# Attention: two chunks' tails transposed into one bank, a fourth p tile, merged tail evictions, another table of turns

## The chip, the cores and the metric

One core of one Trainium2 chip. The metric is the device time of one launch in microseconds (us). Three runs of the kernel before gave 1039.3 to 1040.34 us, median 1039.94 us.

## The reference, cut to what matters

Four batches of eight heads, 576 positions, head size 64, all float32; then two dense blocks.

```python
def _attn_ref(q, k, v, tau):
    scores = q @ k.T / sqrt(64)                       # per head, 576 x 576
    thresh = max(scores, -1) - tau
    scores = where(scores >= thresh, scores, -1e9)
    attn = exp(scores - max(scores, -1))
    attn = attn / (sum(attn, -1) + 1e-9)
    return attn @ v
x = attention output as (4 * 576, 512)
h = x @ w_in;  g = max(h, 0) + alpha * min(h, 0);  x = g @ w_out      # d_ff 2048
x = (((x @ w1) * (x @ w2)) @ w3) @ w_out2                              # d_ff 1024
```

The weights of the dense blocks come as float64 and are turned into float32 on the chip by integer operations.

## The kernel before, in words

The kernel has two stages, each written out by a planner in Python as one fixed list of instructions per engine. The first, attention, ends near 306 us; the dense stage fills the rest. The change touches the first, and of the second only where two weight tiles lie.

Attention goes over 16 pairs of heads (P). The 576 queries of a pair are cut into chunks of 128: chunks 0 to 3 for each of the two heads (units 0 to 7, chunk c of head h is unit 2c+h), and the last 64 queries of both heads together as unit 8. A step has a letter and a number:

- a, b, c, d: load of q or k, split into two fp32r parts on GpSimd (POOL), transposition on TensorE (PE; cq, ck, and ctails for the last 64 positions of both), eviction on ScalarE (ACT; dq, dk, dtails; prep_ev, lines 304 to 331). dswap makes the second form of q by two DMAs.
- Q: four matmuls of scores (eight for unit 8) into one of three two-bank PSUM tiles "s", which cq and ck use too. R: row maximum on VectorE (DVE). H: threshold. E: exp on ACT. M: mask and multiply on DVE into a p tile, of which there are NPB = 3; M frees the s tile.
- G (POOL) and I (DVE): the reciprocal of the sum. C: scaling of p on POOL, in place.
- T: transposition of p on PE, with the PSUM tag "ptp" (two banks) that ctails and V use too. Chunk c has three groups: g = 0 and 1, four blocks of 128 columns for either head, and g = 2, the one block that holds the last 64 columns of both heads. Txg is named after the chunk's second unit: T10, T11, T12 for chunk 0, T30.. for chunk 1, T50.. for 2, T70.. for 3, T80 and T82 for unit 8. X: its eviction on ACT (trans_ev, lines 493 to 509).
- V0, V1: 20 matmul calls of p against v for chunks 0 and 1, then for chunks 2, 3 and the last 64. Y: eviction into xT.
- w0 to w8: conversion of 14 tiles of w_in in the shade of attention: w0 load (512 KB on the SP queue, one buffer), w1 on ACT, w2 to w5 on DVE, w6 on POOL, w7 on ACT, w8 on POOL.

Each step has a number in the table AT (line 578); its turn is that number plus PER times the pair. turn_order (lines 87 to 118) takes, of the steps whose inputs are already in the list, the one of the lowest turn; a step that takes a tile waits in it until the tile's former holder is freed. Every engine runs its part of this list in order, and so does the SP queue with its DMAs.

SBUF: xT and the 16 tiles "wa" lie on the left, the attention pool on the right. That pool is closed after attention, and the dense stage's buffers ("raw" among them) take its place.

Of the kernel before, what the change touches and what calls it, by code (L numbers as in the profile page):

```python
# [120 lines left out]
def kernel(  # L121
# [99 lines left out]
    with tc.manual_schedule():  # L221
# [26 lines left out]
        for i in range(2):  # L248
# [83 lines left out]

# [1205 lines left out]
```

## Time and profile before

| | |
|---|---|
| median of three runs | 1039.94 us |
| the profiled execution | 1039.72 us |
| its span, first to last instruction | 1037.9 us |
| PE, DVE, ACT, POOL busy | 1014.1, 751.6, 580.6, 340.1 us |
| mean granted clock of TensorE | 0.998 |

The page gives busy time over the whole span, which hides that two stages are added up; the views by window below show the attention stage alone. A PE record holds the time until the matmul's modelled end, so that records of PE overlap; on DVE and ACT the records of neighbours overlap too, and what one more instruction costs is the distance of two starts.

### The profile page before, as it was taken

Reading aid. Unit: us, or ns where it says so; the run is one execution under the profiler, and the core shown is the slowest. Engines: PE = TensorE matmul, PEld = TensorE weight load, DVE = VectorE, ACT = ScalarE, POOL = GpSimd, SP = SyncE. Lnnn points to the kernel's source line nnn. Section 1 sums busy time; section 2 is a strip of 40 time slices with the busy share of each in tenths; the row PEclk is TensorE's granted clock in tenths of the full one; section 3 lists DMA queues with packets and bytes.
Section 4 is the critical chain, followed back from the end, with each engine's and each line's share of the span. In section 5 each row is a group of like instructions: output and inputs, shape, how many; then the busy total and the mean of one; then the engine's idle time right before and its main releaser. Section 6 shows DMA issues by size and latency. Waiting matters only on the chain.

```text
span 1037.9 us, 16931 instructions
## 1 busy us (share of the span) xinstructions
PE 1014.1 (98%) x5870; PEld 867.0 (84%) x5870; DVE 751.6 (72%) x1556; ACT 580.6 (56%) x1119; POOL 340.1 (33%) x469
## 2 busy tenths in 40 slices
PE   8999999999989999999999999999999999999997
PEld 6778777777858889988888888888899999999997
DVE  7999999999858787667656565638475587577554
ACT  5998989999865665544443344324143363345331
POOL 4888888888733232222211211103200000000000
PEclk9999999999999999999999999999999999999999
DMA  5353443435113333434524233512242233224201
GB/s 128 90 141 100 131 112 117 125 89 153 39 41 104 112 110 114 141 117 156 176 80 142 104 136 106 172 41 72 92 139 75 81 108 122 71 72 148 91 11 61
DMA packets 71445, 109.50 MB, mean 106 GB/s; under 512 B 14912, under 2 KB 43584, under 8 KB 71360
## 3 DMA queue, kind: packets, MB, share of 16 engines
q1 hardware_dynamic: 68992, 108.16, 33.3%
q8 instruction: 46, 0.75, 0.3%
q10 hardware_dynamic: 2368, 0.27, 0.2%
q14 instruction: 39, 0.32, 0.1%
HBM read 80.22 MB, written 18.35 MB: 95 GB/s over the span
## 4 chain that ended last, share of the span: by engine, by line
PE 87%; POOL 5%; issue 2%; DVE 2%; ACT 2%; DMA 1%; SPq 0%; POOLq 0%; ACTq 0%; DVEq 0%
PE h L985 25%; PE acc L985 24%; PE h L1341 17%; PE pv_ps L518 8%; PE pt_ps L491 5%; PE s_ps L402 5%; POOL p L474 3%; PE tr L291 2%; POOL ks L181 1%; POOL qs L181 1%; PE zero L352 1%; PE h L858 1%; DMA raw<-in_moe_w_dram 0%; POOL praw L474 0%; ACT qT L311 0%
## 5 line engine op out<-in xcount | busy, mean ns | idle before, releaser
L985 PE MATMUL h<-x,wa 128*128 128x512 f32 (+1 forms) x960 | 212.4, 371 | 1.1 <-ACT x L183 1.1
L985 PE MATMUL acc<-gs,wu 128*128 128x512 f32 (+1 forms) x960 | 209.8, 368 | 0.4 <-DVE wu L829 0.4
L985 PEld LDWEIGHTS h<-x,wa 128*128 128x128 f32 x960 | 167.3, 189 | 32.6 <-ACT x L183 3.0
L985 PEld LDWEIGHTS acc<-gs,wu 128*128 128x128 f32 x960 | 168.1, 189 | 31.0 <-DVE wu L829 0.8
L1341 PE MATMUL h<-T,sw 128*128 128x384 f32 x1008 | 190.6, 336 | 0.0
L1341 PEld LDWEIGHTS h<-T,sw 128*128 128x128 f32 x1008 | 178.4, 188 | 8.3
L218 POOL TENSOR_TENSOR m<-m,raw 128x512 int32<-128x512 int32 x58 | 81.6, 1408 | 281.5 <-DVE m L213 213.9
L1405 DVE TENSOR_TENSOR ct<-h,ct 128x384 f32<-128x384 f32 x120 | 66.8, 557 | 91.6 <-PE h L1341 91.5
L426 DVE TENSOR_REDUCE sm<-s_ps 128x1 f32<-128x576 f32 x144 | 105.6, 751 | 13.2 <-PE s_ps L402 13.1
L437 ACT ACTIVATE e<-s_ps,sm 128x576 f32<-128x576 f32 x144 | 106.0, 764 | 7.4 <-DVE sm L426 4.7
L474 POOL TENSOR_SCALAR p<-p,sm 128x576 f32<-128x576 f32 x128 | 96.7, 762 | 26.8 <-DVE sm L467 17.7
L451 DVE SCALAR_TENSOR_TENSOR p<-s_ps,sm,e 128x576 f32<-128x576 f32 x128 | 102.6, 811 | 0.8 <-ACT e L437 0.8
L183 ACT CAST gs<-g 128x512 fp32r<-128x512 f32 (+1 forms) x80 | 46.2, 577 | 94.2 <-PE acc L985 77.5
L491 PE MATMUL pt_ps<-ident,p 128*128 128x128 f32 x576 | 87.3, 280 | 11.3 <-ACT pt L505 8.7
L188 DVE TENSOR_TENSOR gs<-g,gs 128x512 fp32r<-128x512 f32 (+1 forms) x80 | 60.0, 750 | 47.0 <-ACT gs L183 46.4
L1056 ACT ACTIVATE g<-h,sign_sb 128x512 f32<-128x512 f32 (+1 forms) x80 | 51.3, 642 | 69.5 <-PE h L985 62.2
L1061 DVE SCALAR_TENSOR_TENSOR g<-h,salpha_sb,g 128x512 f32<-128x512 f32 (+1 forms) x80 | 55.6, 694 | 47.3 <-ACT g L1056 47.2
L491 PEld LDWEIGHTS pt_ps<-ident,p 128*128 128x128 f32 x576 | 66.0, 142 | 26.5 <-POOL praw L474 10.5
L518 PE MATMUL pv_ps<-pt,vraw 128*64 128x256 f32 (+1 forms) x640 | 84.7, 411 | 0.3 <-ACT xT L531 0.2
L183 ACT CAST sw<-w 128x512 fp32r<-128x512 f32 (+1 forms) x96 | 54.0, 569 | 55.4 <-PE h L1341 53.6
L505 ACT COPY pt<-pt_ps 128x512 f32<-128x512 f32 x128 | 74.5, 596 | 15.6 <-PE pt_ps L491 14.6
L985 PE MATMUL acc<-wp,x 128*128 128x512 f32 x288 | 81.9, 394 | 0.0
(121 smaller groups left out, 1521.3 us busy)
## 6 DMA issues: line engine op xcount, KB each, us to landing
raw<-in_moe_w_dram SPq DMA_DIRECT2D x32, 512.0 KB, 3.7
raw<-in_moe_w_out_dram SPq DMA_DIRECT2D x24, 512.0 KB, 3.5
w<-w SPq DMA_DIRECT2D x48, 256.0 KB, 2.6
qU<-qT SPq DMA_DIRECT2D x30, 320.0 KB, 4.0
w<-w SPq DMA_DIRECT2D x24, 384.0 KB, 2.9
wraw<-in_moe_w_in_dram SPq DMA_DIRECT2D x14, 512.0 KB, 3.8
w<-m SPq DMA_DIRECT2D x24, 256.0 KB, 2.1
z<-w SPq DMA_DIRECT2D x24, 256.0 KB, 2.7
```

The costliest lines, as they stand in the source:

```text
L183: eng.copy(out=dst, in_=src)
L218: nc.gpsimd.tensor_tensor(out=mc[0], in0=mc[0], in1=mc[1], op=ALU.add)
L426: nc.vector.tensor_reduce(out=sm_of(u, 0), in_=st[u], axis=AX.XY, op=ALU.max, negate=True)
L437: nc.scalar.activation(out=es[u].rearrange("p (j s) -> p j s", j=2), in_=st[u], func=AF.Exp, bias=sm_of(u, 0))
L451: nc.vector.scalar_tensor_tensor(out=p_at(u).rearrange("p (j s) -> p j s", j=2), in0=st.pop(u), scalar=sm_of(u, 1), in1=es.pop(u).rearrang ...
L474: nc.gpsimd.tensor_scalar(out=out, in0=in_, scalar1=sm_of(u, 3), scalar2=1.0, op0=ALU.mult, op1=ALU.mult)
L491: nc.tensor.transpose(t[:, i, :], p[:, at + i * 128 : at + (i + 1) * 128], ident)
L505: nc.scalar.copy(out=pt[:, g, 0:4, to], in_=ps)
L518: nc.tensor.matmul(out=o[64 * hh : 64 * hh + 64, 0:n], lhsT=vr[:, hh, i, :], rhs=pt[:, 0 if i == 4 and not half else hh, i, :], start=(i = ...
L985: nc.tensor.matmul(out=out, lhsT=l, rhs=r, start=first and i == 0, stop=last and i == n - 1)
L1341: nc.tensor.matmul(out=bank_()[:, 0:HT], lhsT=w()[:, ap_, kc * 128 : kc * 128 + 128], rhs=x()[:, bp, kc * HT : kc * HT + HT], start=first ...
L1405: lambda e: ENG[e].tensor_tensor(out=dst(), in0=x(), in1=y(), op=how),
```

## The change

Five edits, and a sixth that follows from the second:

1. The blocks g = 2 of chunks 0 and 1 (and of 2 and 3) are transposed in one step into one bank, and evicted by one copy (128x256, or 128x512 with the doubling) where there were two. T12, X12, T52, X52 are gone; T32 waits for the scaling of chunks 0 and 1, T72 for that of 2 and 3.
2. NPB is 4.
3. dtails: one copy for q (128x128) and one scaled copy for k (128x256), where there were two each.
4. w2 of the 14 tiles goes from DVE to ACT.
5. AT has other numbers.
6. "wa" has 14 tiles; the two last w_in tiles of the dense stage lie in a pool "w_b" opened after attention at the place of the two dropped.

```diff
-    w_a = wa_ctx.enter_context(tc.tile_pool(name="w_a", bufs=16, reuse_waits="tile"))
+    w_a = wa_ctx.enter_context(tc.tile_pool(name="w_a", bufs=14, reuse_waits="tile"))
...
-        NPB = 3
+        NPB = 4
...
-                for h in range(2):
-                    nc.scalar.copy(
-                        out=d["qT"][:, h, SM + ST * h : SM + ST * h + ST],
-                        in_=ps[:, 0, ST * h : ST * h + ST].bitcast(F32),
-                    )
-                for at in (0, S):
-                    nc.scalar.activation(
-                        out=d["kT"][:, :, at : at + ST],
...
+                nc.scalar.copy(out=tails(d["qT"])[:, SM // ST :: SM // ST + 3, :], in_=by_head(ps[:, 0, :]))
+                nc.scalar.activation(
+                    out=d["kT"].rearrange("p h (b s) -> p h b s", s=ST)[:, :, :: S // ST, :],
+                    in_=by_head(ps[:, 1, :]).unsqueeze(2).to_broadcast([128, 2, 2, ST]),
+                    func=AF.Copy,
+                    scale=kscale,
+                )
...
+            if g == 2:
+                for i, c_ in enumerate((c,) if c == 4 else (c - 1, c)):
+                    nc.tensor.transpose(t[:, i, :], p_of[P, c_][:, SM : SM + 128], ident)
+                return
...
-            elif half == 0:
-                nc.scalar.copy(out=pt[:, 0, 4, to], in_=ps[:, 0])
             else:
-                nc.scalar.copy(out=pt[:, :, 4, to], in_=ps[:, 0].unsqueeze(1).to_broadcast([128, 2, 128]))
+                two = ps[:, 0:2].rearrange("p i s -> p (i s)")
+                if half == 0:
+                    nc.scalar.copy(out=pt[:, 0, 4, 0:256], in_=two)
+                else:
+                    nc.scalar.copy(out=pt[:, :, 4, 0:256], in_=two.unsqueeze(1).to_broadcast([128, 2, 256]))
...
-                    "V",
+                    "V" if i else "A",
                     lambda e, f=f, i=i: high_w_in(e, f, i),
...
+        w_b = wa_ctx.enter_context(tc.tile_pool(name="w_b", bufs=2, reuse_waits="tile"))
```

The two tables are too long to print. What they come to, by the rule of turn_order, is this order per frame (one pair's worth of steps in the steady part; b is the pair before a, n the one after, z the one before b; in the new table PER is unchanged and 14 frames carry w steps, two pairs later than before):

```
before  PE    V1z T10b Q6b T11b Q7b T50b T12b Q0a T52b T51b Q8a T80b T82b Q4a T32b T30b Q1a T31b T70b Q5a T71b V0b cq_n T72b ctails_n Q2a Q3a ck_n
after   PE    V1z Q7b T50b T51b Q0a T11b T31b Q8a T32b T30b Q1a T80b T82b Q4a T72b T70b Q5a V0b ctails_n cq_n ck_n T71b Q2a Q3a T10a Q6a
after   DVE   R7b H6 M6 R0a H0 H7 M7b R8a I7b M0a w5 H8 M8a R1 H1 R4 H4 R5 M1 M4 I1 H5 M5 I8 R2 R3 H3 I5 R6 H2 M2 M3 w3 w4 I3
after   ACT   Y1z X50b X51b E7b X11b X31b E0a X32b X30b E8a X80b X82b X72b X70b w7 E1 E4 E5 Y0b dtails_n dq_n dk_n X71b E2 X10a E3 w2 w1 E6a
after   POOL  C8b G7b C7b C6b w6 bk_n (4) G8a G1a C0a C1a G5a w8 bq (4, the pair after n) C4a C5a G3a C3a C2a
after   SP    aq, w0, dswap_n, v_n, ak (the pair after n)
```

## Rows read from the trace of the kernel before

**Rows 1.** Busy time of each engine in one frame (--windows; columns in the first line)

```profile
core 0: us, PE busy (x) PEld busy (x) DVE busy (x) ACT busy (x) POOL busy (x), PEclk, DMA share, GB/s
136.00:154.00 18.00, 17.29 (x141) 14.08 (x140) 17.03 (x46) 16.33 (x36) 15.54 (x26) 1.00 0.42 117
```

**Rows 2.** Chain that ended last, in one frame: start us, us, what

```profile
138.94 0.54 PE s_ps L402 x4
139.48 0.87 PE pt_ps L491 x8
...
141.32 2.31 PE pv_ps L518 x20
143.63 0.81 PE tr L291 x8
...
145.83 0.65 PE tr L291 x8
```

**Rows 3.** Chain that ended last: first V0, V0 of pair 14, last V1

```profile
33.40 2.31 PE pv_ps L518 x20
...
284.60 2.31 PE pv_ps L518 x20
...
303.64 2.94 PE pv_ps L518 x20
```

**Rows 4.** Timeline, DVE in one frame: start us, us, engine line op

```profile
145.33 1.42 DVE L426 TENSOR_REDUCE sm<-s_ps 128x1 f32<-128x576 f32 x2 [0.71 <-PE s_ps L402]
...
147.23 0.51 DVE L207 TENSOR_SCALAR m<-m 128x512 f32<-128x512 f32 x1
...
148.52 0.32 DVE L429 TENSOR_SCALAR sm<-sm,ctau 128x1 f32<-128x1 f32 x2
...
149.57 0.69 DVE L213 SCALAR_TENSOR_TENSOR m<-wraw,m 128x512 int32<-128x512 int32 x1
...
152.60 0.82 DVE L451 SCALAR_TENSOR_TENSOR p<-s_ps,sm,e 128x576 f32<-128x576 f32 x1
...
153.34 0.21 DVE L429 TENSOR_SCALAR sm<-sm,ctau 128x1 f32<-128x1 f32 x1
...
153.47 0.75 DVE L426 TENSOR_REDUCE sm<-s_ps 128x1 f32<-128x576 f32 x1
```

**Rows 5.** Groups by line, 0 to 345 us: count, busy us, mean ns, idle before

```profile
L313 ACT ACTIVATE kT<-tr,kscale 128x1024 fp32r<-128x1024 f32 x16 | 18.6, 1159 | 0.7 <-PE tr L291 0.7
...
L311 ACT CAST qT<-tr 128x1024 fp32r<-128x1024 f32 x16 | 16.3, 1016 | 9.9 <-PE tr L291 9.9
...
L509 ACT COPY pt<-pt_ps 128x256 f32<-128x256 f32 x32 | 12.4, 387 | 0.0
...
L507 ACT COPY pt<-pt_ps 128x128 f32<-128x128 f32 x32 | 8.9, 279 | 0.4 <-PE pt_ps L491 0.4
...
L204 DVE TENSOR_SCALAR m<-wraw 128x512 int32<-128x512 int32 x14 | 7.4, 529 | 0.4 <-DMA wraw<-in_moe_w_in_dram 0.4
...
L202 ACT ACTIVATE m<-raw 128x512 f32<-128x512 f32 x8 | 5.3, 661 | 0.0
```

**Rows 6.** Timeline, ACT and POOL instructions that follow without a gap

```profile
139.96 1.08 ACT L505 COPY pt<-pt_ps 128x512 f32<-128x512 f32 x2 [0.38 <-PE pt_ps L491]
...
140.92 2.02 ACT L437 ACTIVATE e<-s_ps,sm 128x576 f32<-128x576 f32 x3
...
142.31 1.55 POOL L188 TENSOR_TENSOR ks<-kraw,ks 128x256 fp32r<-128x256 f32 x2
...
153.79 1.47 POOL L474 TENSOR_SCALAR p<-p,sm 128x576 f32<-128x576 f32 x2
```

**Rows 7.** Timeline, start of the dense stage: the same DVE form beside POOL and alone

```profile
310.79 0.43 DVE L209 TENSOR_SCALAR m<-m 128x512 int32<-128x512 int32 x1
...
312.18 1.30 POOL L218 TENSOR_TENSOR m<-m,raw 128x512 int32<-128x512 int32 x1 [14.02 <-DVE m L213]
312.31 1.45 DVE L209 TENSOR_SCALAR m<-m 128x512 int32<-128x512 int32 x1
```

**Rows 8.** DMA issues on the page: KB each, median us to landing

```profile
wraw<-in_moe_w_in_dram SPq DMA_DIRECT2D x14, 512.0 KB, 3.8
```

More of the change, by code (lines that the diff above doesn't have):

```diff
@@ L487, in trans @@
             t = pt_ps[P, c, g] = ps_a.tile([128, 4, 128], F32, tag="ptp", name="pt_ps", bufs=2)
+            if g == 2:
+                for i, c_ in enumerate((c,) if c == 4 else (c - 1, c)):
+                    nc.tensor.transpose(t[:, i, :], p_of[P, c_][:, SM : SM + 128], ident)
+                return
             p = p_of[P, c]
-            at = (0, S + ST, SM)[g]
-            for i in range(1 if g == 2 else 4):
+            at = (0, S + ST)[g]
+            for i in range(4):
                 nc.tensor.transpose(t[:, i, :], p[:, at + i * 128 : at + (i + 1) * 128], ident)
@@ new lines @@
+        AT = {'aq_0': 57.932, 'bq0hi_0': -5.26462375720813e+233, 'bq0lo_0': -5.26462375720813e+233, 'bq1hi_0': -5.264623757208129e+233, 'bq1lo_0': -5.264623757208129e+233, 'ak_0': 72.92, 'bk0hi_0': 0.526, 'bk0lo_0': -5.264623757208129e+233, 'bk1hi_0': 6.578, 'bk1lo_0': -1.7211269975488118e+233, 'cq_0': 21.681, 'dq_0': -3.479850037031599e+233, 'ctails_0': 113.869, 'dtails_0': -5.200977034580411e+233, 'ck_0': 124.257, 'dk_0': -5.200977034580411e+233, 'eq': 125.223, 'fq': -5.264623757208129e+233, 'etails': 130.148, 'ftails': 140.709, 'v': 131.775, 'Q0': -20.437, 'R0': 134.255, 'H0': -5.26462375720813e+233, 'E0': -5.200977034580411e+233, 'M0': 136.284, 'Q1': 130.138, 'R1': 138.618, 'H1': -5.264623757208129e+233, 'E1': -5.200977034580411e+233, 'M1': 140.689, 'G1': -1128612512929.835, 'I1': 141.951, 'C0': -1128612513286.866, 'C1': -1128612513124.268, 'T10': 145.941, 'X10': -8.744473794239729e+233, 'T11': 152.259, 'X11': -5.200977034580411e+233, 'Q2': 145.25, 'R2': -5.26462375720813e+233, 'H2': 149.291, 'E2': -5.200977034580411e+233, 'M2': -5.26462375720813e+233, 'Q3': 145.874, 'R3': 146.402, 'H3': 140.522, 'E3': -5.200977034580411e+233, 'M3': -1.7211269975488118e+233, 'G3': -1128612513645.092, 'I3': 151.42, 'C2': 154.089, 'C3': -1128612513643.817, 'T30': 130.66, 'X30': -5.200977034580411e+233, 'T31': 153.127, 'X31': -5.200977034580411e+233, 'T32': 126.195, 'X32': -5.200977034580411e+233, 'V0': 161.753, 'Y0': -5.200977034580411e+233, 'Q4': 130.67, 'R4': 138.658, 'H4': -5.264623757208129e+233, 'E4': -5.200977034580411e+233, 'M4': 141.226, 'Q5': 130.827, 'R5': 140.629, 'H5': 142.561, 'E5': -5.200977034580411e+233, 'M5': -6.985750754756941e+233, 'G5': -1128612512933.779, 'I5': 146.948, 'C4': -1128612513642.171, 'C5': -1128612513477.898, 'T50': 150.728, 'X50': -5.200977034580411e+233, 'T51': 130.128, 'X51': -5.200977034580411e+233, 'Q6': 148.891, 'R6': -5.264623757208129e+233, 'H6': 153.805, 'E6': -5.200977034580411e+233, 'M6': 5.684, 'Q7': 150.608, 'R7': 152.245, 'H7': 154.281, 'E7': -5.200977034580411e+233, 'M7': -5.264623757208129e+233, 'G7': 155.923, 'I7': -5.264623757208129e+233, 'C6': 156.493, 'C7': -1128612513645.102, 'T70': 127.236, 'X70': -5.200977034580411e+233, 'T71': 164.241, 'X71': -8.744473794239729e+233, 'T72': 126.185, 'X72': -5.200977034580411e+233, 'Q8': 123.723, 'R8': 134.922, 'H8': 138.246, 'E8': -5.200977034580411e+233, 'M8': -5.264623757208129e+233, 'G8': -1128612512580.549, 'I8': 143.079, 'C8': 155.831, 'T80': 114.406, 'X80': -3.479850037031599e+233, 'T82': 150.618, 'X82': -5.200977034580411e+233, 'V1': 168.997, 'Y1': -5.200977034580411e+233, 'aq': 87.91, 'bq0hi': -1128612512927.751, 'bq0lo': -1128612513123.155, 'bq1hi': -1128612512933.769, 'bq1lo': -1128612512739.518, 'ak': 117.955, 'bk0hi': -1128612514737.118, 'bk0lo': -1128612513308.768, 'bk1hi': -1128612513645.112, 'bk1lo': -1128612515450.783, 'cq': 124.058, 'dq': -5.200977034580411e+233, 'ctails': 123.77, 'dtails': -5.200977034580411e+233, 'ck': 124.596, 'dk': -3.479850037031599e+233, 'dswap': 131.139, 'w0': 167.278, 'w1': -5.200977034580411e+233, 'w2': -6.922104032129223e+233, 'w3': 169.511, 'w4': -5.26462375720813e+233, 'w5': 176.358, 'w6': -1128612514734.24, 'w7': -5.200977034580411e+233, 'w8': 182.722, 'z1': 123.949, 'z2': 128.359, 'z3': 116.205}
@@ L683 @@
                 ]
-                groups = ((0, Cs), (2, Cs)) if j == 8 else ((0, Cs[:1]), (1, Cs[1:]), (2, Cs))
-                for g, src in groups:
+                if j == 8:
+                    groups = ((0, Cs, ms[:1]), (2, Cs, ms[:1]))
+                elif j in (1, 5):
+                    groups = ((0, Cs[:1], ms[:1]), (1, Cs[1:], ms[:1]))
+                    early = Cs, ms[:1]
+                else:
+                    groups = ((0, Cs[:1], ms[:1]), (1, Cs[1:], ms[:1]), (2, early[0] + Cs, early[1] + ms[:1]))
+                for g, src, done in groups:
                     new = j in (1, 5) and g == 0
@@ L693 @@
                         take="ptp",
-                        free=ms[:1],
+                        free=done,
                     )
@@ L1022 @@
                 w_in_k.append(by_k(box))
-                w_in_ops.append([halves(box, a, first, 5.2 * f - 8, w_a, "wa")])
+                w_in_ops.append([halves(box, a, first, 5.2 * f - 8, w_b, "wb")])
             box, a, first = weight(rows(w_out, f), 5.2 * f + 2)
```

11 lines of the change are left out of this document (4 added, 7 removed).

## The prediction

> **What bounds the kernel now.** I read the busy times by window first, since the page adds two stages up. One frame of attention [rows 1] has PE at 17.29 of 18 us, DVE at 17.03, ACT at 16.33, POOL at 15.54: no engine stands out, and all four wait a little. The reader should see that a price taken off one of them buys nothing by itself; what counts is the longest closed loop of steps through two or three of them.
>
> Second, the chain that ended last. In the steady part it is nearly all PE, and its pieces give PE's prices [rows 2]: a unit of scores Q 0.54, eight transposed blocks 0.87 (so 0.44 for a T of four and 0.11 for a block), V0 2.31, eight transpositions of q or k 0.81 behind V and 0.65 behind Q. By these a frame asks PE for 40 score matmuls (10 x 0.54 = 5.4), 41 blocks (4.5), V0 and V1 (2.3 + 2.9 [rows 2, 3]) and cq, ck, ctails (0.81 + 0.65 + two of sixteen, 0.16 = 1.6): 16.7. The rest of its 17.29 is the tail of a record that nothing follows at once.
>
> Third, the same chain over the whole of attention [rows 3]: first V0 at 33.40, V0 of pair 14 at 284.60, so 14 frames of (284.60 - 33.40) / 14 = 17.94. The last V1 ends at 303.64 + 2.94 = 306.58, 21.98 after that V0. What follows to the end of the span is 1037.9 - 306.58 = 731.3.
>
> So a frame lasts 17.94 where the busiest engines need 16.7 to 17.0, and the change can win some of 1.2 us, 14 times.
>
> **The change part by part.**
>
> *w2 to ACT.* DVE loses 0.53 a frame, 17.03 to 16.50; ACT gets the same operation at 0.66 [rows 5]. ACT records overlap by about a tenth (DVE: 0.82 recorded against 152.60 to 153.34 = 0.74 from start to start [rows 4]), so it costs some 0.56. w2 is put behind E3, ahead of w1 and E6, and adds a wait for the weight's DMA there: behind it stand w1, E6 and Y1, for which M6 and T51 wait. The load takes 3.8 us [rows 8]; on SP it goes out when w6 of the tile before is done, before bk, V0 and cq of the same frame, while w2 comes after dq, dk, X71, E2, X10 and E3. By the durations below that is bk 2.4, ctails and cq 1.0, and 4.6 for dq to E3: 8.0, some 4 to spare. If the cover were gone, each us would be paid in each of 14 frames.
>
> *Merged tails and dtails.* Two copies of 128x128 (2 x 0.28) become one of 128x256 (0.39); two of 128x256 (0.77) become one of 128x512, 0.54 by the pair in [rows 6]; four pieces of dtails become two. With the overlap, that takes 0.3 off ACT a frame (0 to 0.7 as bounds: nothing if the wider access patterns, which no row shows, cost more, and the whole recorded difference). ACT: 16.33 + 0.56 - 0.3 = 16.6. PE transposes as many blocks as before, but takes "ptp" 15 times a frame and not 17, so two waits for an eviction are gone. The new wait: T32 and T72 need the scalings of two chunks. Behind T72 stand T70, Q5 and V0; C7 and C6 leave POOL right before w6, well ahead of T72 as counted below.
>
> *Fourth p tile.* It holds the earlier chunk until its late tail; without it M of the next chunk would wait on T32 and T72. I cost both together at nothing.
>
> *The table.* DVE, ACT, POOL, PE and SP get new orders; as printed with the change, I add up the longest loops through them.
>
> DVE and PE: from R7 to M8 DVE does 3 R, 4 M, 4 H, one I, w5 without a gap; then Q5, V0, ctails, cq, ck, T71, Q2 on PE; then R2 to I3 on DVE (3 R, 2 M, 2 H, 2 I, w3, w4), and R7 again. R is 0.67 (two in 1.42, one record 0.75), M 0.74, H 0.13 (153.34 to 153.47), I the same, w5 0.69, w3 and w4 148.52 - 147.23 = 1.29 [rows 4]. First part 2.01 + 2.96 + 0.65 + 0.69 = 6.31; third 2.01 + 1.48 + 0.52 + 1.29 = 5.30; PE 0.54 + 2.31 + 1.62 + 0.44 + 0.54 = 5.45 [rows 2]. Two hand-offs at 0.25 each are an estimate (R at 145.33 starts 0.1 after the end of its Q in the chain; the other way I allow 0.4). Sum 17.56.
>
> w3 and w4 are what can be smaller. The same form took 0.43 alone and 1.45 beside a POOL instruction of 1.30 [rows 7]. In the new order POOL has only G3 to do when they run: G3 waits for M3, C3 for I3, which is behind w4. At 0.43 each the loop is 17.56 - 0.43 = 17.13. The Trainium skill, "SBUF — State Buffer", section "SBUF: two separate sides", says that VectorE and GpSimd share a pair of ports as an exclusive lock, held for a whole instruction while the loser waits. The row agrees: 312.31 + 1.45 is 0.28 after the end of the POOL instruction that started 0.13 earlier. By that rule the loop is 17.13, provided POOL is idle there; by the prices of the old neighbourhood, 17.56.
>
> POOL beside it: from I7, C7 and C6 (1.47), w6 (1.30), the four bk (1.55 for the lower parts [rows 6], some 0.85 for the upper) are 5.2, and then ctails. In the same stretch the first loop does M0, w5, H8, M8, Q5, V0 and a hand-off: 0.74 + 0.69 + 0.13 + 0.74 + 0.54 + 2.31 + 0.25 = 5.4. POOL is just not later.
>
> ACT and PE: dq 1.02, dk 1.16 [rows 5], X71, E2, X10, E3, w2, w1, E6, Y1; T51; X51, E7, X11, X31, E0, X32, X30, E8, X80; T72, T70, Q5, V0, ctails, cq. With E at 2.02 / 3 = 0.67 and X at 0.54 [rows 6]: 6 E 4.0, 7 X 3.8, X32 0.4, w1 and w2 1.3, Y1 0.45, dq and dk 2.2, PE 0.44 + 0.22 + 0.44 + 0.54 + 2.31 + 0.97 = 4.9, four hand-offs 1.0: 18.1 by records, and 17.0 to 17.6 with a tenth of overlap for five to ten of them.
>
> *SP.* w0, about two pairs later, stands between aq and dswap; dswap needs dq and has from there to Q0 of the next frame, some 6 us. v waits for V1 and ak behind it; the kraw it brings is wanted on POOL after w6 of the next frame. I see no stall, with about 2 us to spare.
>
> Three loops lie at 17.0 to 17.6. I take 17.4, near the two that use the old prices, because POOL's idle moment beside w3 is the one assumption I can't check.
>
> *Start.* The first frame has no w steps any more (w3, w4, w5: 1.98 [rows 4]), and DVE is what it waits for; I take 1.9: first V0 at 31.5. Ends: 0 (PE's 16.7 bind instead) and 2.5.
>
> *Drain.* The last tiles' w steps now fall into frame 14 and the scaling after it, but the frames without them before were the last two; T71 and X71 now stand between the last V0 and V1 (0.44 + 0.54 + hand-offs, some 1.0), and PE has no ctails and cq there. I leave it at 21.98, ends -2 and +1.
>
> *"wa" and "w_b".* Same conversions, same list of the dense stage, the same place as the two dropped tiles: nothing. The place of "raw" slides over other p tiles, released before or after the last V0: within 1 us either way.
>
> Sum: 31.5 + 14 x 17.4 = 275.1, against 284.60; + 21.98 + 731.3 = 1028.4 span; the profiled execution adds 1039.72 - 1037.9 = 1.8: **1030.2**. That execution is 0.2 below the median of the runs, which I leave as it is.
>
> **The rivals.**
>
> *Loops near the floors.* w3 and w4 at 0.43, ACT records overlapping as fully as the 16.33 busy suggests: frame 17.0, 5.6 less, and a drain 1 shorter: 1023.6. For it: three engines at 16.5 to 16.7 and the POOL gap. Against: three full engines in fixed orders rarely stay so close.
>
> *The steady part is not better.* ACT, now at 16.6, makes PE wait as it did, and the frame stays 17.94: only the start's 1.9 is won, and something at the drain's ends: 1037.8. For it: the order before, too, was 1.2 above its floors.
>
> *ACT takes the bound and the time is longer.* The ACT loop by records, 18.1, holds because w2 in front of w1 and E6 puts Y1, and with it T51 and all PE work behind it, late in every frame. Price 0.16 x 14 = 2.2, less the start's 1.9, plus 1 at the drain; with the load 0.2 late as well, 2.8 more: 1041 to 1044. It decides from a frame of 18.1 up. For it: ACT is the one engine that gets work. Against: its records do overlap.
>
> *It doesn't do what it says*: a step stands elsewhere than I read it, or the moved tiles hold back the dense stage's first weight loads. 0 to 3 on top of the forecast, some 1032.
>
> **How the numbers follow.** Forecast (frames of 17.2 to 17.8, 1027 to 1036) 0.55; near the floors 0.17; no better 0.13; longer 0.10; not as it says 0.05. The range 1024.5 to 1037.5 leaves out about 1 in 10 on either side. The measurement tells 0.2%, 2.1 us: faster than 1037.8 has the first two, the last, and about a quarter of "no better", 0.80; within 0.2% the rest of that, 0.10; slower 0.10.
>
> **What would show it.** V0 to V0 at 17.4 from about 31.5 on, DVE busy near 16.5 a frame and ACT near 16.6; DVE without a gap from R2 to M8 and one wait of about 1 us ahead of R2; w3 and w4 at 0.43 (then 17.1) or 0.51 and 0.83; no wait of w2 on its DMA; the dense stage 731 long. Frames of 18 or more, ACT without any gap, or a stall of T32 or T72 on POOL would make the forecast wrong.

## The result, and the profile after

The changed kernel takes 1051.8 us (1051.7 to 1053.0) beside 1039.7 of the kernel before in the same series: ratio 1.0119, interval 1.0101 to 1.0136. It is slower by 1.2%, where 1030.2 was forecast, 0.9% faster than before. Its span is 1049.7, 21.3 above the 1028.4 of the forecast.

The span can be taken apart as the forecast's was. The chain of waits has (answering to [rows 3]; start us, us, what):

```profile
33.81 0.79 PE pv_ps L521 x5
...
316.05 3.59 PE pv_ps L521 x20
```

V0 of pair 14 isn't in this chain. TensorE's timeline has it; there a V0 starts 0.07 earlier than in the chain (the first at 33.74):

```profile
297.69 2.38 PE L521 MATMUL pv_ps<-pt,vraw 128*64 128x256 f32 x20
```

The first V0 starts at 33.81 (forecast 31.5), the mean of 14 frames is (297.69 - 33.74) / 14 = 18.85, and a steady one takes 18.91 (forecast 17.4, before 17.98 from V0 to V0 in the same stretch). The last V1 ends at 319.64, 21.9 after V0 of pair 14 (forecast 21.98), and what follows lasts 1049.7 - 319.64 = 730.1 (forecast 731.3). So of the 21.3 us, 14 x 1.45 = 20.3 are the frame and 2.3 the start; drain and dense stage give 1.3 back. The frame is what has to be explained. Its busy times, in the columns of [rows 1]:

```profile
166.11:185.02 18.91, 18.16 (x141) 14.12 (x143) 17.13 (x46) 16.65 (x32) 15.85 (x26) 1.00 0.39 111
```

ScalarE stands at 16.65, as forecast. VectorE should have lost the 0.53 of w2 and stands at 17.13, 0.1 above before. GpSimd has no step more than before and 0.3 more busy time. So steps got longer, on two engines. VectorE's timeline of this frame (as [rows 4]) shows which:

```profile
171.35 1.42 DVE L423 TENSOR_REDUCE sm<-s_ps 128x1 f32<-128x576 f32 x2 [0.97 <-PE s_ps L399]
...
175.46 0.58 DVE L207 TENSOR_SCALAR m<-m 128x512 f32<-128x512 f32 x1
176.07 0.86 DVE L209 TENSOR_SCALAR m<-m 128x512 int32<-128x512 int32 x1
...
177.09 0.74 DVE L423 TENSOR_REDUCE sm<-s_ps 128x1 f32<-128x576 f32 x1
177.74 0.21 DVE L426 TENSOR_SCALAR sm<-sm,ctau 128x1 f32<-128x1 f32 x1
178.05 0.82 DVE L448 SCALAR_TENSOR_TENSOR p<-s_ps,sm,e 128x576 f32<-128x576 f32 x1
178.80 0.75 DVE L423 TENSOR_REDUCE sm<-s_ps 128x1 f32<-128x576 f32 x1
179.59 0.34 DVE L426 TENSOR_SCALAR sm<-sm,ctau 128x1 f32<-128x1 f32 x2
180.03 0.82 DVE L448 SCALAR_TENSOR_TENSOR p<-s_ps,sm,e 128x576 f32<-128x576 f32 x1
...
182.23 0.82 DVE L213 SCALAR_TENSOR_TENSOR m<-wraw,m 128x512 int32<-128x512 int32 x1
182.97 0.20 DVE L426 TENSOR_SCALAR sm<-sm,ctau 128x1 f32<-128x1 f32 x1
183.31 0.82 DVE L448 SCALAR_TENSOR_TENSOR praw<-s_ps,sm,e 128x576 f32<-128x576 f32 x1
...
184.05 0.75 DVE L423 TENSOR_REDUCE sm<-s_ps 128x1 f32<-128x576 f32 x1
```

171.35 is R2 with R3, 175.46 and 176.07 are w3 and w4; then R7, H6, M6, R0, the pair H0 and H7, M7; then w5, H8, M8, and R1 behind it. The reader should look at the distances of starts. H6 to M6, which reads H6's result, is 0.31, and H8 to M8 0.34; in [rows 4] H is followed by the next step after 0.13, where that step reads something else. R0 to H0, which reads R0, is 0.79; an R has a pitch of 0.67 where another step follows. The new table puts each of the nine H right behind its R or right ahead of its M; in the order before one pair, H8 and M8, stands so. And w3 and w4 last 0.58 and 0.86, w5 0.82 where [rows 4] have 0.69. On GpSimd, the scalings C0 and C1, C4 and C5, C7 and C6 of the frame:

```profile
169.44 1.49 POOL L471 TENSOR_SCALAR p<-p,sm 128x576 f32<-128x576 f32 x2 [0.41 <-PE tr L291]
...
175.00 1.65 POOL L471 TENSOR_SCALAR p<-p,sm 128x576 f32<-128x576 f32 x2
...
181.77 1.90 POOL L471 TENSOR_SCALAR p<-p,sm 128x576 f32<-128x576 f32 x2 [0.63 <-DVE sm L464]
```

They are the same work, 1.47 in [rows 6]: 1.49 where VectorE does none of w3 to w5, 1.65 beside w3 and w4, 1.90 beside w5. The steps of the change itself cost about what was forecast, w2 on ScalarE 703 ns a record (661 in [rows 5]) and the merged evictions 587 and 380 (answering to [rows 5]):

```profile
L202 ACT ACTIVATE m<-wraw 128x512 f32<-128x512 f32 x14 | 9.8, 703 | 0.0
L512 ACT COPY pt<-pt_ps 128x512 f32<-128x512 f32 x16 | 9.4, 587 | 16.5 <-PE pt_ps L487 16.5
L510 ACT COPY pt<-pt_ps 128x256 f32<-128x256 f32 x16 | 6.1, 380 | 1.6
```

Last the chain of waits through the frame, from G5 by w8, the upper and lower bq (not shown), and C4, C5 to I3, and at its end by w5 and C6 to T72, for which TensorE waits with T70, Q5 and V0 behind it:

```profile
171.02 0.19 POOL sm L459
...
171.29 1.28 POOL wa L188
...
175.02 1.63 POOL p L471 x2
...
177.01 0.17 DVE sm L464
...
182.32 0.74 DVE m L213
...
183.09 0.58 POOL p L471
...
183.72 0.33 PE pt_ps L487
```

### The profile page after: what moved, and what is told of

The parts are those of the page before. It is cut to its first block, busy times and chain, and to the rows that moved or that the text cites. A ratio compares the mean times of both kernels' runs of the same rounds, so it can differ in the third digit from the quotient of the medians.

```text
span 1049.7 us, 16763 instructions
## 1 busy us (share of the span) xinstructions
PE 1024.5 (98%) x5870; PEld 867.1 (83%) x5870; DVE 757.0 (72%) x1542; ACT 583.9 (56%) x1069; POOL 344.2 (33%) x469
## 4 chain that ended last, share of the span: by engine, by line
PE 76%; DVE 11%; POOL 8%; issue 2%; ACT 1%; DMA 0%; SPq 0%; DVEq 0%; POOLq 0%; ACTq 0%
PE h L995 25%; PE acc L995 25%; PE h L1351 17%; DVE p L448 4%; PE pv_ps L521 4%; POOL p L471 4%; DVE sm L423 3%; POOL qs L188 2%; PE tr L291 2%; POOL wa L188 1%; PE s_ps L399 1%; DVE m L213 1%; PE pt_ps L492 1%; POOL qs L181 1%; DVE sm L426 1%
## 5 line engine op out<-in xcount | busy, mean ns | idle before, releaser
L995 PE MATMUL h<-x,wa 128*128 128x512 f32 (+1 forms) x840 | 185.4, 370 | 1.2 <-ACT x L183 1.1
L995 PEld LDWEIGHTS h<-x,wa 128*128 128x128 f32 x840 | 146.4, 189 | 28.4 <-ACT x L183 2.7
L471 POOL TENSOR_SCALAR p<-p,sm 128x576 f32<-128x576 f32 x128 | 102.5, 813 | 23.6 <-DVE sm L464 15.4
L188 DVE TENSOR_TENSOR gs<-g,gs 128x512 fp32r<-128x512 f32 (+1 forms) x80 | 62.4, 779 | 47.0 <-ACT gs L183 46.6
L399 PE MATMUL s_ps<-kT,qT 128*128 128x288 f32 x320 | 80.2, 332 | 7.9 <-DVE p L448 4.6
L506 ACT COPY pt<-pt_ps 128x512 f32<-128x512 f32 x128 | 72.1, 589 | 13.0 <-PE pt_ps L492 12.1
L492 PE MATMUL pt_ps<-ident,p 128*128 128x128 f32 x512 | 73.9, 275 | 0.5 <-ACT pt L506 0.3
```

The lines of the kernel that those rows point to most:

```text
L188: eng.tensor_tensor(out=dst, in0=src, in1=hi.bitcast(F32), op=ALU.subtract)
L399: nc.tensor.matmul(out=sp[:, j, 0:HS], lhsT=d[t][:, hh, c * 128 : (c + 1) * 128], rhs=d["kT"][:, hh, k0 + j * HS : k0 + (j + 1) * HS], sta ...
L471: nc.gpsimd.tensor_scalar(out=out, in0=in_, scalar1=sm_of(u, 3), scalar2=1.0, op0=ALU.mult, op1=ALU.mult)
L995: nc.tensor.matmul(out=out, lhsT=l, rhs=r, start=first and i == 0, stop=last and i == n - 1)
```

## The experiments

Four causes were on the list. D is the name for the dependent neighbours (H next to its R or M), K for VectorE's w3, w4, w5 and GpSimd's scalings holding each other up, L for G3 being late behind C4 and C5, W for w2 on ScalarE. Frames are from V0 to V0 in the steady part. Ratios are to the kernel before in the same series. e7, e8 and e9 leave out the conversion of the upper part of 14 weight tiles, so they measure a cause and can't be used as kernels.

**The change taken apart: e1, e2, e3.** e1 has all edits of the change and the old AT:

```diff
-        AT = {... the table of the change ...}
+        AT = {... the table before ...}
```

> The kernel after with the table of turns of the kernel before; all other edits stay (merged tails, merged dtails, four p tiles, w2 on ACT, 14 + 2 weight tiles). Theory D (the new table puts DVE steps right behind the one they read, H behind its R and M behind its H, some 0.15 us each, six of them in the loop that closes a frame): the table is at fault and the edits are a gain, so the frame (V0 to V0, 18.9 after, 18.0 before) is 17.5 to 17.9 and the time 1032 to 1039. Rival W (w2 on ACT makes exps late): frame over 18.2, time over 1042. Rivals L (the new order of POOL makes I3 late on DVE) and K (DVE and POOL hold each other up at w3, w4, w5) expect the same as D here.

1071.3 us, ratio 1.0312 (1.0282 to 1.0342); frame 20.17. The waits from 100 to 300 us (engine line, waited for: us in total, times, longest):

```profile
POOL p L471 <- DVE sm L464: 31.3, 13, 2.7
...
DVE m L207 <- ACT m L202: 20.1, 10, 2.0
```

w3 waits up to 2 us for w2, which the old table puts late in ScalarE's line, and the scalings wait for the I behind w3. The time lies far above the 1032 to 1039 of D, and in the range of W (over 1042): in this order w2 comes late and is waited for. The edits don't fit the old order; what each is worth in a better one came last (e15 to e18).

e2 has the new table, the fourth p tile and "w_b", but tails, dtails and w2 as before:

> The other half: the new table and the four p tiles, but the instructions of before (tails of each chunk transposed and evicted apart, just ahead of the merged step's turn; dtails in four pieces; w2 on DVE). D, L and K: no better than after, frame 18.9 to 19.6 (w2 adds 0.53 to DVE inside the loop), time 1050 to 1060. W: frame near 18, time near 1040.

1067.1 us, 1.0272 (1.0242 to 1.0301); frame 19.68. That is above all expected ranges, and 15 us more than the table with the edits takes: the two belong together.

e3 is the change with w2 back on VectorE:

```diff
-                    "V" if i else "A",
+                    "V",
```

> The kernel after with w2 back on DVE, all else as after. D and K: w2 stands in the loop ahead of w3, frame 19.2 to 19.5, time 1054 to 1058. W: frame back to about 18, time near 1040. L: I3 waits for POOL whatever DVE does before it, frame 18.9 to 19.1, time 1050 to 1053.

1056.2 us, 1.0167 (1.0137 to 1.0196), frame 19.06. W falls for the new table: with w2 on ScalarE the changed kernel is 4.4 us faster than without, so that edit is a gain.

**D and K, each alone and both: e4, e7, e9.** e4 moves the nine H by one to three places, so that another step stands between R and H and between H and M; nothing else changes:

```diff
+            for h, anchor in (("H6", "I3"), ("H7", "M6"), ("H8", "M0"), ("H1", "R4"), ("H4", "R5"),
+                              ("H5", "M1"), ("H2", "R3"), ("H3", "R6")):
+                put((h, P), (anchor, P))
+            put(("H0", P), ("M7", P - 1))
```

> The kernel after with the nine H of a frame moved by one to three places in DVE's order, so that another step stands between R and H and between H and M; nothing else moved. D: the six waits in the loop go, 0.7 to 1.0 us a frame: frame 17.9 to 18.2, time 1037 to 1041. L: I3 still waits for G3, at most 0.2 gained, frame 18.7 or more, time over 1047. K: no gain, 1050 or more.

1045.7 us, 1.0061 (1.0038 to 1.0084); frame 18.48. D is real, and with 0.43 a frame about half the expected size. VectorE's timeline, H7, R0, M7:

```profile
176.00 0.21 DVE L426 TENSOR_SCALAR sm<-sm,ctau 128x1 f32<-128x1 f32 x1
176.12 0.75 DVE L423 TENSOR_REDUCE sm<-s_ps 128x1 f32<-128x576 f32 x1
176.79 0.81 DVE L448 SCALAR_TENSOR_TENSOR p<-s_ps,sm,e 128x576 f32<-128x576 f32 x1
```

H to R takes 0.12 and R to the M of another unit 0.67. But the scalings C4, C5 (1.65 in the changed kernel) and C7, C6 are as long as they were or longer, so the 0.43 is what D gives less what C4 and C5 take back:

```profile
172.20 1.90 POOL L471 TENSOR_SCALAR p<-p,sm 128x576 f32<-128x576 f32 x2
...
178.63 1.89 POOL L471 TENSOR_SCALAR p<-p,sm 128x576 f32<-128x576 f32 x2 [0.75 <-DVE sm L464]
```

e7 leaves H where the change has it and puts reductions of one operand, about as long, in the place of w3, w4 and w5:

```diff
+                nc.vector.tensor_reduce(
+                    out=red[:, i : i + 1], in_=wa["m", f].bitcast(F32)[:, 0:n], axis=AX.X, op=ALU.max
+                )
```

> The kernel after with w3, w4 and w5 replaced by reductions of the m tile that read one operand (300, 300 and 512 elements, about as long as w3, w4, w5 without a neighbour) into a scratch; the 14 w_in tiles are left unconverted. K: pairs of scalings back to 1.48, w3 and w4 at 0.45 each, frame 18.0 to 18.4, time 1036 to 1043. D and L without K: nothing, frame 18.8 or more, time over 1047.

1048.1 us, 1.0081 (1.0052 to 1.011); frame 18.53, 0.38 less, where K expected 0.5 to 0.9. The reductions also take less of VectorE (16.39 busy a frame, 17.13 in the changed kernel), but that isn't what the loop gains ahead of I3: VectorE now waits 0.49 there for G3. All pairs of scalings take 1.47 or 1.48. e9 has both:

> The changed kernel with two things together: the nine H moved so that no step stands directly behind the one it reads (as in the run with H alone moved: 18.48 us a frame), and w3, w4, w5 replaced by reductions of one operand of about the same length, so that they don't hold up GpSimd's scalings (14 w_in tiles stay unconverted in their upper part). G3 stays where the new table has it. Theory (dependent neighbours and shared ports, side by side): the two gains of the single runs, .43 and .38 a frame, add up or do better, since both lie on one loop: frame 17.3 to 18.1, 1030 to 1041 us, and the wait of T72 for C6 (.35 + .33 in the run with H alone) is under .2. Rival (they are the same wait seen twice): frame 18.3 to 18.5, 1043 to 1046 us. Rival (G3 behind C4, C5 still makes I3 late): I3 shows an idle time of over .5 and the frame stays over 18.1.

1035.1 us, 0.9958 (0.9941 to 0.9974), and a frame of 17.7:

```profile
158.44:176.11 17.67, 17.62 (x141) 14.10 (x140) 15.58 (x45) 16.38 (x32) 15.17 (x26) 1.00 0.44 118
```

The two together give 1.2 a frame, more than 0.43 + 0.38: either alone leaves the other's wait on the loop. The four runs make a square. With the reductions in, H apart is worth 0.84 (18.53 to 17.69), and this is the cleaner price of D, as no scaling changes its length between e7 and e9; with H apart, the reductions are worth 0.79 (18.48 to 17.69). That 0.79 is GpSimd's side of K: VectorE waits 0.92 (e4) and 0.97 (e9) for G3, so w3 and w4 aren't on the loop, w5 and what stands for it take 0.61 and 0.59, and the pairs C4, C5 and C7, C6 shorten from 1.90 and 1.89 to 1.48 each. Both causes together win 16.7 of the 21.6 us between forecast and result. The rest shows in e9's chain of waits, where one loop closes by itself, from G5 to the next G5, 181.00 - 163.31 = 17.69:

```profile
163.31 0.19 POOL sm L459
...
167.32 1.46 POOL p L471 x2
...
169.09 0.17 DVE sm L464
...
181.00 0.19 POOL sm L459
```

5.78 of it are GpSimd's, from G5 to I3 by w8, bq, C4, C5 (now 1.46) and G3; 10.2 are VectorE's from I3 to I1; the rest is C0, C1.

**D on the old table: e10.** The kernel before, each H moved right behind its R:

```diff
+            for j in range(9):
+                put((f"H{j}", P), (f"R{j}", P))
```

> The kernel before, its own table and instructions, with one thing moved: each of the nine H of a frame stands directly behind the R whose result it reads. Nothing that another engine waits for comes later but by this. Theory (dependent neighbours): R to H takes .79 in place of .67, nine times, less the one H right ahead of its M that this takes apart (.2): .9 us more of VectorE's work a frame, on the loop that bounds it; frame 18.4 to 18.9 from 17.98, 1045 to 1053 us. Rival (the order of H costs nothing by itself; the new table's loss is in other waits): R to H stays at .67, 1038 to 1041 us.

1051.1 us, 1.0115 (1.0099 to 1.013); frame 18.85, 0.87 longer, where 0.9 was expected. First w3, then R, H and the step behind:

```profile
154.22 0.84 DVE L207 TENSOR_SCALAR m<-m 128x512 f32<-128x512 f32 x1
...
160.62 0.75 DVE L426 TENSOR_REDUCE sm<-s_ps 128x1 f32<-128x576 f32 x1
161.41 0.21 DVE L429 TENSOR_SCALAR sm<-sm,ctau 128x1 f32<-128x1 f32 x1
161.54 0.81 DVE L451 SCALAR_TENSOR_TENSOR p<-s_ps,sm,e 128x576 f32<-128x576 f32 x1
```

R to H 0.79, H to a step that doesn't read it 0.13: the price is the one read after the change. But the 0.87 isn't D's alone, and that it meets the 0.9 is in part luck. w3 takes 0.84 in this run where [rows 4] have 0.51, since it now lies beside other GpSimd steps; it stands on the chain of waits, so some 0.3 of the 0.87 are w3's and not D's.

**L: e5, e6, e8.** G3 moved from behind C5 to right behind M3, ahead of C4 and C5; e5 on e4, e6 on the change, e8 on e9:

```diff
+            put(("G3", P), ("M3", P))
+            put(("C4", P), ("G3", P))
+            put(("C5", P), ("C4", P))
```

> As e4 (H apart; frame 18.48), and on POOL the small step G3 goes ahead of the two scalings C4, C5 that stood before it; nothing else moves. Theory L (what is left of the loss is I3 at the head of DVE's queue, waiting some 0.9 us for G3 behind C4 and C5): frame 17.4 to 17.8, time 1030 to 1037. Theory K (ports shared by DVE and POOL: scalings take 1.9 a pair beside w3, w4, w5 where they take 1.48 alone, and that sets the loop): at most 0.2 gained, frame 18.2 to 18.5, time over 1041.

> The kernel after with G3 ahead of C4, C5 and H where the new table has it. Theory D (dependent neighbours on DVE close the frame by themselves): I3 is hardly waited for there, frame 18.7 to 18.9, time 1046 to 1050. Theory L alone: frame 18.0 to 18.3, time 1037 to 1042.

> All three at once: H apart, G3 early, reductions in place of w3, w4, w5 (the 14 w_in tiles left unconverted). If D, L and K are the whole of it, the frame is what the forecast's loops gave, 17.0 to 17.4, and the time 1024 to 1030. If something else is in it, 17.6 or more, time over 1032.

e5 1049.1 us (1.0091, 1.0061 to 1.012), e6 1060.1 (1.0196, 1.0167 to 1.0226), e8 1039.6 (1.0002, 0.999 to 1.0013). None gains on the run without the move: the frames are 18.51, 19.07 and 17.8 against 18.48, 18.91 and 17.69, so L falls, for which e5 had expected 17.4 to 17.8 and e6 18.0 to 18.3. The times are 3.4, 8.3 and 4.5 us longer, mostly by the start and the first and last frames (in e6 the first V0 comes 3.6 later). I3 comes sooner, but C4 and C5 wait for M3, and TensorE's T51 for them.

**Can the order alone win it back: e11, e12, e13, e17.** All are e4 with more moved, nothing left out. e11 puts w5 behind M8:

> The run with H apart, with w5 behind M8 in place of ahead of it (and H8 behind I7), so that the scalings C7, C6 run for the most part beside no step that locks the port. Theory (shared ports): C7, C6 take 1.5 to 1.6 in place of 1.89, T72's second transpose waits .3 less, and the frame falls from 18.48 to 18.1 to 18.3: 1040 to 1043.5 us. Rival (the scalings' length isn't on the loop; w5 late makes w6 and then C0, C1 late): 1045 to 1048 us.

1050.7 us, 1.011 (1.0095 to 1.0125). The scalings became as short as expected, the time got longer than even the rival had it. GpSimd's C7, C6 and then w6:

```profile
180.01 1.48 POOL L471 TENSOR_SCALAR p<-p,sm 128x576 f32<-128x576 f32 x2 [0.75 <-DVE sm L426]
...
182.35 1.30 POOL L218 TENSOR_TENSOR m<-m,wraw 128x512 int32<-128x512 int32 x1 [0.86 <-issue]
```

C7 and C6 take 1.48 without w5 beside them; then GpSimd stands still for 0.86, since w6 needs w5, and all behind it is late.

e12 puts V0 ahead of T72 and T70 on TensorE, so that it covers the wait for C6, and w7 behind E4:

> The run with H apart, with V0 moved ahead of T72 and T70 on TensorE (it reads nothing of them), so that its 2.3 us cover the wait for C6; T72, cq, T70 follow, X72 and X70 behind Y0 on ScalarE, and w7 behind E4. Theory (what is left over 17.6 in the run with H apart is TensorE's wait for C6, .35 + .33, itself made by the ports and the dependent steps): frame 17.7 to 18.1, 1034 to 1041 us, no wait of T72 for C6. Rival (the loop runs through GpSimd and VectorE, C0, C1 to G5, w8, C4, C5, G3, I3, and TensorE's wait is only where it shows): frame 18.3 to 18.6, 1043 to 1047 us, the wait turns up ahead of another matmul.

1047.0 us, 1.0077 (1.0062 to 1.0092): the rival. The wait turns up at Q5, for M8.

e13 puts R7 ahead of I3, into VectorE's wait of 0.92 for G3:

```diff
+            put(("I3", P), ("R7", P))
+            put(("C3", P), ("I3", P))
```

> The run with H apart (18.48 us a frame), with R7 moved ahead of I3 on VectorE: there I3 waits .92 for G3 while R7's scores are complete at 173.3, a us before it runs. The computation is complete. Theory (a single loop through VectorE and GpSimd with its waits sets the new table's time; a step put into the wait shortens it): all from M6 on comes .7 earlier, I7 and with it C7, C6 too, so T72's wait of .35 goes; frame 17.7 to 18.0, 1034 to 1039 us. Rival (M6's exponential or a bank for Q7, not VectorE's place in line, holds that stretch): frame 18.3 to 18.5, 1043 to 1046 us.

1042.0 us, 1.0025 (1.0016 to 1.0034); frame 18.17. Half of what was expected: 0.3 a frame; the wait moves to the scalings C4, C5 and T51 behind them. e17 adds w5 behind I3 and I7 ahead of R8:

> The run with H apart and R7 ahead of I3 (18.17 us a frame), with w5 moved behind I3, so that it runs beside the scalings C3, C2, for which TensorE doesn't wait, and not beside C7, C6; and I7 ahead of R8, so that C7 starts sooner. The computation is complete. Theory (shared ports: C7, C6 take 1.5 in place of 1.90, T72's second transpose doesn't wait): frame 17.8 to 18.0, 1035 to 1040 us. Rival (the loop through C4, C5 beside w3 and w4, then T51, sets the frame; C7, C6 have no part in it): 18.1 to 18.3, 1040 to 1044 us.

1041.8 us, 1.0024 (1.0016 to 1.0033): no change against e13, the rival. C3, C2, now beside w5, and C7, C6:

```profile
171.15 1.85 POOL L471 TENSOR_SCALAR p<-p,sm 128x576 f32<-128x576 f32 x2 [0.30 <-DVE sm L464]
...
174.79 1.48 POOL L471 TENSOR_SCALAR p<-p,sm 128x576 f32<-128x576 f32 x2 [0.37 <-PE pt_ps L492]
```

The lengthening goes where w5 goes, and the 0.4 is paid there: the frame has few stretches in which GpSimd is free. With H apart and R7 moved, the change is 10 us faster than it was, and still 2 us behind the kernel before.

**The edits on the old table: e14, e15, e16, e18.** e14 is the kernel before with H2, H3, M2, G5 and I5 ahead of w2 to w5:

> The kernel before with I5 (and G5, H2, H3, M2 ahead of it) moved ahead of the four steps w2 to w5, which in its frame hold I5 back to 150.18 while GpSimd's scaling C4 waits 1.22 for it. The computation is complete and no step is added. Theory (what counts in these frames is which step stands ahead of what GpSimd and TensorE wait for): C4 to C2 come 1.0 to 1.2 earlier and TensorE's waits of .57 and .3 behind them go: frame 17.3 to 17.7 from 17.98, 1029 to 1036 us. Rival (TensorE's waits there are for ScalarE's evictions alone, which don't come earlier): 1038 to 1041 us.

1046.3 us, 1.0064 (1.0049 to 1.0079). I5 did come sooner, but w2, w3, w4, w5 in a row, each reading the one before it and beside GpSimd's work (w3 0.86 in place of 0.51), hold M3, R6, E6 and an eviction behind it that TensorE waits for. A miss. e15 adds w2 on ScalarE:

> The run before this one, and w2 on ScalarE behind w1 (from the second w_in tile on; the first one's at the start): the one edit of the change that the run with w2 back on VectorE showed to be a gain (4.4 us). Theory: VectorE's loop loses .5, ScalarE stands at 17.0 of the frame; if TensorE is the bound by then the gain is small: 17.2 to 17.6 a frame, 1027 to 1034 us. Rival (ScalarE's evictions of E3, dk and Y1 come .6 later and TensorE waits for them, as the old table has nothing to cover it): as e14 or slower, 1036 to 1045 us.

1043.2 us, 1.0036 (1.0024 to 1.0049): w2 on ScalarE is a gain of 3.1 here too. e16 is the kernel before with w2 on ScalarE behind E2, and VectorE's line in another order:

```diff
- R2 R3 w2 w3 w4 H2 H3 M2 w5 I5 M3
+ R2 R3 H2 H3 M2 w3 w4 I5 M3 w5
```

> The kernel before, its tails and evictions as they were, with w2 on ScalarE behind E2 (but for the first w_in tile), and VectorE's order R2, R3, H2, H3, M2, w3, w4, I5, M3, w5 in place of R2, R3, w2, w3, w4, H2, H3, M2, w5, I5, M3: unlike in the run with I5 ahead of w2 to w5, M3 isn't behind w5, and comes 1.2 earlier than in the kernel before. Theory (w2 is worth .55 of VectorE's loop wherever ScalarE has the room; e15 over e14 showed 3.1 us): frame 17.4 to 17.8 from 17.98, 1031 to 1038 us. Rival (E3 behind w2 and w1 comes .6 later, M3 and what follows wait for it, or C4 beside w4 and w5 grows as in e14): 1039 to 1045 us.

1035.5 us (1035.3 to 1037.1), 0.9964 (0.9951 to 0.9978): 3.9 us faster than the kernel before, with the whole computation. Frame 17.73. Its chain of waits is nearly all TensorE, with one stretch through ScalarE (T11, X11 and E6, X50, then T52 and T51; X50 not shown):

```profile
167.09 0.62 PE pt_ps L491 x4
...
167.73 0.59 ACT pt L505
...
169.58 0.73 PE pt_ps L491 x5
```

e18 adds to e16 the merged tails, the merged dtails and the fourth p tile, that is, all instruction edits of the change in a good old order (three steps are put by hand where e16 has them, so that the order differs only by T12, T52 and their evictions):

> All instruction edits of the change (merged tails T32 and T72, one eviction for each, merged tails of the next pair, four p tiles, w2 on ScalarE) in the old table's order as the run e16 has it (17.73 us a frame, 1035.5 us): the two differ by the tails alone, T12 and T52 going into T32 and T72. Theory (the edits are a gain, the new table is what failed): ScalarE loses two evictions of about .2 and two of the next pair's tails, TensorE has two banks fewer to wait for among T50, T12, T52, T51, where it waits for ScalarE now: frame 17.2 to 17.6, 1028 to 1034 us. Rival (the merged tails bring nothing here, as no wait ends on the two small evictions): 1034.5 to 1037 us. Rival (the run with the old table and all edits, 1071 us, was slow by the tails and not by w2's place): over 1040 us.

1043.0 us, 1.0034 (1.0021 to 1.0046), 7.5 slower than e16; frame 18.23. Both the theory and its mild rival missed, and the time is in the range of the second rival, that the late tails cost. They explain 7.5 us, and not the 32 by which e1 is above the kernel before. The waits from 100 to 300 us:

```profile
PE s_ps L399 <- DVE p L448: 6.8, 22, 0.4
DVE p L448 <- PE pt_ps L487: 6.0, 11, 0.6
```

M0 waits in every frame, 0.55 each, for T32 (L487), which holds the p tile of the earlier chunk until then, and Q1 waits for M0; e16 has no such wait of M0. ScalarE does save what was forecast (16.58 busy a frame in e16, 16.29 here), and that is paid by a tile that comes free later.

## Why the prediction was wrong

*The step that failed* is the frame's loops, of which 17.56 for VectorE and TensorE was the longest. "From R7 to M8 DVE does 3 R, 4 M, 4 H, one I, w5 without a gap" was right, at 0.13 for H and 0.67 for R it was not. That stretch takes 184.05 - 177.09 = 6.96 in place of 6.31: two H right ahead of their M, one R right ahead of its H, the pair H0 and H7 right ahead of M7, and w5. The loop's other terms were short too: R2 to I3 took 177.09 - 171.35 = 5.74 in place of 5.30, again with an H right ahead of its M and an R right ahead of its H, and with 1.55 from w3 to I3 in place of 1.29; TensorE's part with its hand-offs took the rest of 18.91, 6.21 in place of 5.95, as T72 waits for C6. So the loop that was priced at 17.56 is the one that measured 18.91, and 0.65, 0.44 and 0.26 are what its three terms were mis-sized by. The old order shows the price: [rows 4] have H as a record of 0.21 and a pitch of 0.13, and the pitch holds only for a next step that doesn't wait for the result. e4, e9 against e7, and the distances in e10 show that this is the price and not something beside it. In the trace before, the one such pair, H8 and M8, lies under a wait for E8. But the price could be read elsewhere in it:

```profile
142.50 0.33 DVE L429 TENSOR_SCALAR sm<-sm,ctau 128x1 f32<-128x1 f32 x2
...
142.81 0.82 DVE L451 SCALAR_TENSOR_TENSOR p<-s_ps,sm,e 128x576 f32<-128x576 f32 x1
```

These are H1 and H5, then M1, which reads H1. M1 starts 0.31 after H1, the same distance as from H6 to M6 after the change, where two H at 0.13 would make 0.26. H2, H3 and M2 stand in the same way at 148.52 and 148.83. The forecast took the 0.13 from a place where the next step reads something else, and gave the other case no bounds.

*The ports.* The forecast saw that w3 and w4 can be longer beside GpSimd [rows 7], took "POOL has only G3 to do when they run", and priced that as a possible gain. C4 and C5 run there: they start when the lower bq ends, and G3 stands behind them. And the price has two sides: the scalings grow by 0.2 to 0.4 a pair, which the forecast did not count anywhere. The Trainium skill, "SBUF — State Buffer", section "SBUF: two separate sides", has the lock as exclusive, with the loser waiting. The traces agree that one waits: 1.90 beside w5, 1.48 where w5 was moved away. That the wait lasts for a whole instruction they don't show, as the pair grows by 0.42 and w5's own record is 0.68 to 0.82.

*"POOL is just not later"* looked at GpSimd from I7 on only. The loop from C0 by G5, w8, bq, C4, C5, G3 to I3 and by VectorE back to I1 was not added up. e9 measures it, free of both other causes, at 17.69. VectorE waits 0.97 for G3 in it, so w3 and w4 are not on it, and what stands for w5 takes 0.59 where the forecast had 0.69: this is why the frame would have missed 17.4 by 0.3 even with the forecast's durations.

*Start.* 33.81 and not 31.5: "DVE is what it waits for" was taken without its chain. Before the change that chain, in the first frame, is SyncE's queue and the load of v:

```profile
21.84 1.68 SPq L376
...
25.25 1.92 DMA vraw<-in_v_dram
```

so leaving out w3 to w5 there bought nothing. Afterwards it runs through VectorE, with R, H, R, H in a row from 15.62 (R to H 0.79 by the timeline) and an H right ahead of its M at 24.12 (0.31). Why SyncE is no longer the one that ends it, while the time is the same, was not tried.

*The fourth p tile and late tails*, "both together at nothing": in the new table that held, as M0 has no wait for T32 there; e18 shows 0.55 a frame where it has.

*What held.* ScalarE's 16.6; w2 as a gain (e3 4.4 us, e15 3.1); no wait of an engine for a load from 100 to 300 us; drain and dense stage. Of the rivals, none was the one that came: "ACT takes the bound" is on the right side for a wrong reason, and "a stall of T32 or T72 on POOL", listed among the signs, is what the chain shows.

What stays open: whether some order of the changed kernel beats e16. Its frame with both causes removed, 17.7, is no better than e16's 17.73, which still has one wait of TensorE for ScalarE.

## What to carry to other kernels

When a new order is priced, price pairs and not steps: for each step ask whether the one right ahead of it on its engine is the one that it reads, and, where steps of two engines lengthen each other, what the other engine does meanwhile. Add up every closed loop, also the ones through an engine that is the least busy. An edit that saves instructions by doing something later also holds a buffer longer; look at who waits for that buffer.

## What the runs showed of the hardware

A VectorE step behind the one whose result it reads starts 0.12 to 0.2 us later than behind another: H to M 0.31 to 0.34 against 0.13, R to H 0.79 against 0.67 (after, e4, e10). One short step between doesn't hide all of it (H1, H5, M1 before: 0.31 from H1 to M1). Setting nine H apart gains 0.84 us a frame where nothing else changes its length (e7 to e9). Two scalings on GpSimd take 1.46 to 1.49 us by themselves, 1.85 to 1.90 beside one w5, and 1.65 (after) to 1.90 (e4) beside w3 and w4; the reductions that took their place in e7 and e9, which read one operand and write one number a partition, lengthen nothing (1.47, 1.48). w3 isn't of one length either: 0.42 in e4, 0.51 before, 0.84 in e10 and 0.86 in e14.
